# Sigmoid attention and a GELU feed-forward on one core: attention units two by two

## The chip, the core and the metric

The kernel runs on one core of one Trainium2 chip. The time is device microseconds of one execution; the kernel before has a median of 1010.88 us in three runs (1010.87 to 1011.01). The profile is one further execution, recorded by the hardware profiler.

Engines are named as the profile names them: PE (TensorE matmul), PEld (its weight loads), DVE (VectorE), ACT (ScalarE), POOL (GpSimd), SP (the queue that issues most loads).

## What is computed

```python
# q, k, v: (8 batches, 12 heads, 448, 64) fp32; w_in 768x2048, w_out 2048x768
scores = scale * np.matmul(q, k.transpose(0, 1, 3, 2)) - np.log(S)
attn = 1.0 / (1.0 + np.exp(-scores))
out = np.matmul(attn, v).astype(np.float32)
x = np.ascontiguousarray(out.transpose(0, 2, 1, 3)).reshape(B * S, H * D)   # 3584 x 768
h = x @ w_in
g = 0.5 * h * (1.0 + erf(h * inv_sqrt2))
return (g @ w_out).astype(np.float32)
```

## The kernel before

The program has two phases on the one core. The attention takes about the first 245 us, the feed-forward the rest. The change is in the attention alone; the feed-forward splits each product into seven smaller ones and stays as it is.

**Units.** Four heads of one batch make a unit; there are 24, three to a batch, and unit u belongs to batch u // 3. For each unit `scores` (L447) makes six score tiles of 128 keys x 2 x 448 queries, two head pairs by three key blocks. Each tile is three steps of two matmuls: q and k are split into a high part `hi` (a cast, L408) and a low part `lo` (raw minus `hi`, L417), and the steps are hi x lo, lo x hi and hi x hi. ACT turns each tile into probabilities with a sigmoid (L425), from PSUM into one of eight SBUF buffers `a`. The last 64 keys of all heads form one more tile, `sc_t` (`scores_tail`, L464), made from unsplit operands.

**Values.** `values(u)` (L480) multiplies probabilities and v into the PSUM tile `pav`, in two halves: first the tail and the three blocks with one wiring of the array's quarters, then the three blocks with the other. Between the halves DVE copies one column of `pav` into `ones`, the program's tile `mark` (L507); the second half waits for that copy. There too stands the score tail of the next unit.

**Parking.** After `values(u)` DVE copies the two halves of `pav` out (`park`, L531). From unit 6 on, each half goes into a buffer of `piece` (names `x6_0`, `x6_1` for unit 6), of which there are three in rotation, and from there by a DMA that POOL issues (L532) to the DRAM tile `scr_x`. Units 0 to 5 are copied mostly straight into SBUF tiles `x0_jk`, in halves (L525, L528).

**PSUM.** There are four tile places (`ps0` to `ps3`) of two banks each. Six score tiles go round over the four; `pav` and the next tail take two of them, and `place` exchanges third and fourth from unit to unit.

**Side work.** During the attention a `Decoder` rebuilds the weights from their raw bits in 20 chunks. A chunk has five steps: scale and place on ACT (L145, L156), a `post` step, then join (DVE, L175 and L183) and round (DVE, L190). Once two chunks are joined, `post` mixes their quarters with four DVE additions (`mix`, L107 to L110) and POOL issues seven DMAs of the results to DRAM (`scr_in`, L210). The table `STEPS` says how many steps come before `values` and how many inside, after the mark: (3, 2) for units 2 to 9 and 11 to 18, then (3, 1), (4, 1), (4, 1), (4, 0) for units 20 to 23. In unit 10 instead of it DVE combines quarters of the finished first rows of x (L564, L565: 128x1344 each), and in unit 19 it makes their low part (L568). `qk`, `v` and the raw weights are loaded by SP into three buffers each.

**Order.** Each engine runs its instructions in the order in which the Python code writes them. For a unit that is: six score tiles, splits of the next unit's q and k on DVE (the first pair's `hi` on ACT, in `idle`, for units up to 17), the decoder's steps, `values` with mark and tail, `park`, the next loads.

Of the kernel before, what the change touches and what calls it, by code (L numbers as in the profile page):

```python
# [17 lines left out]
P = 128  # L18
# [4 lines left out]
def tile_sigmoid_attention_gelu_ffn(  # L23
# [88 lines left out]

    def piece(name):
        return sb.tile([P, S], F32, tag="tmp", name=name, bufs=3)
# [7 lines left out]
    class Decoder:  # L122
        def __init__(self):
            self.raws, self.parts, self.rest, self.out = {}, {}, {}, None
            self.done = self.groups = self.closed = 0
            self.mixing, self.pending, self.open, self.second = [], [], [], None
            self.queue, self.next = nc.sync, None
            self.steps = self.work()
            self.taken = 0

# [69 lines left out]
        def post(self):  # L200
            some = bool(self.mixing or self.pending and self.second)
            while self.mixing:
                j, a = self.mixing.pop()
                s = sb.tile([P, 2, WU], F32R, tag="whl", name=f"sin{j}", bufs=WHL)
                s = s.bitcast(F32).rearrange("p a b -> p (a b)")
# [25 lines left out]
        def work(self):  # L231
# [3 lines left out]
            for i in range(len(CHUNKS)):  # L235
                self.scale(i)
                yield True
                self.place(i)
                yield True
# [8 lines left out]
            yield self.post()  # L248

# [20 lines left out]
    LATE = 17  # L270
    STEPS = {u: (3, 2) for u in (*range(2, 10), *range(11, 19))}
    STEPS |= {20: (3, 1), 21: (4, 1), 22: (4, 1), 23: (4, 0)}
    STEPS_IN_ALL = 5 * len(CHUNKS) + 2

    class Weights:
# [25 lines left out]
        def load_to(self, n, must=False):  # L301
            while self.loaded < min(n, len(self.units)):
# [4 lines left out]
                t = sb.tile([P, WU], F32, tag="wst", name=f"wst{i}", bufs=WST)  # L307
# [4 lines left out]
        def high_to(self, n):  # L312
            while self.ready < min(n, len(self.units)):
# [4 lines left out]
                hl = sb.tile([P, 2, WU], F32R, tag="whl", name=f"whl{i}", bufs=WHL)  # L318
# [55 lines left out]
    def attention(at, ps):  # L374
        raws, vals, parts, probs, pavs = {}, {}, {}, {}, {}
        total = B * NU

        def load(u):
            if u >= total:
                return  # L380
            b, n = divmod(u, NU)
# [36 lines left out]

        def sigmoid(u, p, c, sc, braided):
            a = at.tile([P, 2, S], F32, tag="a", name=f"a{u}_{p}_{c}", bufs=8)  # L420
            to = a
            if braided:
                to = a.rearrange("p j (a b) -> p j a b", a=2)
                sc = sc.rearrange("p j (b a) -> p j a b", a=2)
            nc.scalar.activation(to, sc, AF.Sigmoid, bias=NEG_LOG_S, scale=SCALE)  # L425
            probs[u, p, c] = a

        def place(u, n, name):
            third, fourth = (2, 3) if u % 2 == 0 else (3, 2)
            i = (0, 1, third, fourth, 0, 1, third, fourth)[n]  # L430
            return ps[max(i - 1, 0)].tile([P, 2, 512], F32, tag=f"ps{i}", name=name)[:, :, :S]

        def scores(u, p, c):
            if u >= total:
                return
            sc = place(u, FULL * p + c, f"sc{u}_{p}_{c}")
# [17 lines left out]
            sigmoid(u, p, c, sc, braided)  # L454
# [3 lines left out]
        def scores_tail(u):  # L458
# [3 lines left out]
            sc = place(max(u - 1, 0), 2 * FULL + 1, f"sc{u}_t")  # L462
# [10 lines left out]
        def values(u, meanwhile, idle):  # L473
            pav = pavs[u] = place(u, 2 * FULL, f"pav{u}")

            def chunk(c, swap):
                a = [probs[u, 0 if c == FULL else p, c] for p in range(2)]
# [11 lines left out]
            order = [0, 1, 2, FULL] if u == 0 else [FULL, 0, 1, 2]  # L489
            if u == total - 1:  # L490
                chunk(FULL, 0)
                for p in range(2):
                    for c in range(FULL):
                        for j in range(2):
# [3 lines left out]
                                probs[u, p, c][:, j],  # L498
# [6 lines left out]
            for c in order:  # L505
                chunk(c, 0)
            nc.vector.tensor_copy(mark, pav[:, :, 0])  # L507
            meanwhile()
            scores_tail(u + 1)
            idle()  # L510
            for c in range(FULL):
                chunk(c, 1)

# [29 lines left out]
        warm = place(0, FULL, "warm")  # L543
# [7 lines left out]
        for u in range(total):  # L551
            for p in range(2):
                for c in range(FULL):
                    scores(u, p, c)
            if u == 0:
                scores_tail(u)
# [5 lines left out]
            if u == 10:  # L562
# [3 lines left out]
            if u == 19:  # L566
# [3 lines left out]
            def meanwhile():  # L570
                if u == 0:
                    split_qk(1, 0)
                    split_qk(1, 1)
                decode(u, 1)
# [3 lines left out]
            def idle():  # L578
                if 2 < u + 2 <= LATE:
                    high_qk(u + 2, 0, nc.scalar.copy)  # L580
                if u == 10:
# [4 lines left out]
            values(u, meanwhile, idle)  # L586
# [7 lines left out]
            if u in (total - 6, total - 5):  # L594
                W.load_to(2 * (u - total + 7))

# [343 lines left out]
```

## Time and profile before

| what | us or share |
|---|---|
| median of three runs | 1010.88 |
| span of the profiled execution | 1009.3 |
| PE busy | 1004.9 (100%) |
| PEld busy | 909.3 (90%) |
| DVE busy | 705.4 (70%) |
| ACT busy | 678.8 (67%) |
| POOL busy | 105.0 (10%) |
| chain that ended last: PE | 95% |
| of it the scores (L447), the values (L480) and the tails (L464) | 9%, 13%, 2% |

The span runs from the first to the last instruction in the record; the run's time is 1.6 us above it. A timeline row gives a start, the time from there to the end of its last instruction, and how many instructions stand in it (xN); a bracket behind it says how long the engine had been idle and what released it. Matmuls overlap, so the difference of two starts says what a stretch costs PE, not the time of one row. One matmul of the order lists below is two records in the trace.

### The profile page before, as it was taken

How to read it: one execution, taken by the hardware profiler on the slowest of the kernel's cores; microseconds unless marked ns; L12 is line 12 of the kernel's file. 1: busy time of each engine (PE TensorE's matmuls, PEld its weight loads, DVE VectorE, ACT ScalarE, POOL GpSimd, SP SyncE). 2: the span in 40 equal slices, each digit the busy share in tenths (PEclk: the TensorE clock that was granted, in tenths of full speed). 3: DMA queues.
4: the chain of work that ended last, by engine and by line, in shares of the span. 5: the costliest groups of instructions: out<-in, count | busy, mean ns of one | idle time of the engine just before them, and what ended most of it. 6: DMA issues, size and time to landing. Idle time of an engine off the chain costs nothing.

```text
span 1009.3 us, 16521 instructions
## 1 busy us (share of the span) xinstructions
PE 1004.9 (100%) x6406; PEld 909.3 (90%) x6406; DVE 705.4 (70%) x834; ACT 678.8 (67%) x935; POOL 105.0 (10%) x168
## 2 busy tenths in 40 slices
PE   9999999999999999999999999999999999999998
PEld 5656666667999999999999999999999999999998
DVE  3677777777988987773378867534887774368873
ACT  5888887788886756567665655766656467666652
POOL 0122222233323210010000000100000000000000
PEclk9999999999999999999999999999999999999999
DMA  9899999998996765564344455634435543334441
GB/s 275 246 333 331 313 323 330 340 346 286 331 332 218 201 236 149 169 198 146 127 120 126 142 148 172 195 115 130 132 112 151 162 145 120 110 110 125 141 140 64
DMA packets 83214, 199.16 MB, mean 197 GB/s; under 512 B 9408, under 2 KB 33984, under 8 KB 83136
## 3 DMA queue, kind: packets, MB, share of 16 engines
q1 hardware_dynamic: 69360, 152.24, 49.3%
q0 software_dynamic: 11840, 39.23, 11.1%
q10 hardware_dynamic: 1936, 6.63, 1.9%
q8 instruction: 50, 0.82, 0.3%
q14 instruction: 28, 0.23, 0.1%
HBM read 156.10 MB, written 41.29 MB: 196 GB/s over the span
## 4 chain that ended last, share of the span: by engine, by line
PE 95%; DVE 2%; issue 2%; DMA 0%; ACT 0%; POOL 0%; DVEq 0%; POOLq 0%
PE pf L602 71%; PE pav L480 13%; PE sc L447 9%; PE sc_t L464 2%; DVE tmp L639 1%; DVE whl L326 0%; PE pav L495 0%; DMA scr_out<-wd 0%; PE warm L545 0%; POOL scr_out L219 0%; DVE wd L175 0%; DVE wd L190 0%; DVE xl_p L639 0%; DVE g L639 0%; ACT me L145 0%
## 5 line engine op out<-in xcount | busy, mean ns | idle before, releaser
L602 PE MATMUL pf<-op,whl 128*128 128x448 f32 x2016 | 382.1, 352 | 0.0
L602 PEld LDWEIGHTS pf<-op,whl 128*128 128x128 f32 x2016 | 380.9, 189 | 0.5 <-DVE op L639 0.2
L602 PE MATMUL pf<-xh_p,whl 128*128 128x448 f32 x1296 | 353.0, 353 | 0.1
L326 DVE TENSOR_TENSOR whl<-wst,whl 128x768 fp32r<-128x768 f32 x224 | 213.5, 954 | 153.6 <-ACT whl L319 153.2
L319 ACT CAST whl<-wst 128x768 fp32r<-128x768 f32 x224 | 186.0, 830 | 142.3 <-PE pf L602 124.5
L602 PEld LDWEIGHTS pf<-xh_p,whl 128*128 128x128 f32 x1296 | 244.9, 189 | 1.4 <-issue 0.7
L602 PE MATMUL pf<-xl_p,whl 128*128 128x448 f32 x624 | 219.9, 352 | 0.0
L425 ACT ACTIVATE a<-sc 128x896 f32<-128x896 f32 x144 | 119.2, 933 | 34.3 <-PE sc L447 34.2
L480 PE MATMUL pav<-a,v 64*64 64x448 f32 x1296 | 133.1, 541 | 0.0
L639 DVE TENSOR_TENSOR op<-g,op 128x896 fp32r<-128x896 f32 x112 | 121.3, 1084 | 0.9 <-ACT op L649 0.9
L602 PEld LDWEIGHTS pf<-xl_p,whl 128*128 128x128 f32 x624 | 117.9, 189 | 0.1
L480 PEld LDWEIGHTS pav<-a,v 64*64 64x64 f32 x1296 | 55.5, 132 | 61.0 <-issue 33.4
L649 ACT CAST op<-g 128x896 fp32r<-128x896 f32 x112 | 104.8, 936 | 1.7 <-PE pf L602 1.7
L639 DVE TENSOR_TENSOR g<-g,g 128x896 f32<-128x896 f32 x64 | 69.3, 1083 | 0.0
L636 ACT ACTIVATE g<-tmp 128x448 f32<-128x448 f32 x64 | 40.3, 631 | 38.2 <-DVE tmp L639 38.1
L636 ACT ACTIVATE g<-pf 128x448 f32<-128x448 f32 x64 | 34.8, 543 | 39.9 <-PE pf L602 39.7
L639 DVE TENSOR_TENSOR tmp<-pf,g 128x448 f32<-128x448 f32 x64 | 39.8, 623 | 26.3 <-PE pf L602 17.8
L351 POOL DMA_DIRECT2D x<-scr_x x24 | 18.0, 807 | 324.8 <-ACT g L746 204.2
L447 PE MATMUL sc<-lo,hi 64*128 64x448 f32 x276 | 51.2, 367 | 0.0
L417 DVE TENSOR_TENSOR lo<-qk,hi 128x896 fp32r<-128x896 f32 x46 | 50.1, 1088 | 1.1
L447 PE MATMUL sc<-hi 64*128 64x448 f32 x276 | 48.7, 349 | 0.0
L447 PE MATMUL sc<-hi,lo 64*128 64x448 f32 x276 | 48.7, 349 | 0.0
(75 smaller groups left out, 746.1 us busy)
## 6 DMA issues: line engine op xcount, KB each, us to landing
wst<-scr_in SPq DMA_DIRECT2D x112, 384.0 KB, 3.1
wst<-scr_out SPq DMA_DIRECT2D x112, 384.0 KB, 3.1
v<-v_dram SPq DMA_DIRECT2D x48, 256.0 KB, 7.9
raw<-w_in_dram SPq DMA_DIRECT2D x16, 767.8 KB, 6.0
out_dram<-tmp SPq DMA_DIRECT2D x47, 224.0 KB, 2.1
qk<-q_dram SPq DMA_DIRECT2D x23, 448.0 KB, 9.7
qk<-k_dram SPq DMA_DIRECT2D x46, 224.0 KB, 10.4
scr_out<-wd POOLq DMA_DIRECT2D x36, 256.0 KB, 5.2
```

What stands on the lines that cost most here:

```text
L319: nc.scalar.copy(hl[:, 0], t)
L326: nc.vector.tensor_tensor(hl[:, 1], t, hl[:, 0], op=ALU.subtract)
L351: queue.dma_start(dst[:, :, a], src[:, :, a])
L417: nc.vector.tensor_tensor(lo, raw, hi, op=ALU.subtract)
L425: nc.scalar.activation(to, sc, AF.Sigmoid, bias=NEG_LOG_S, scale=SCALE)
L447: nc.tensor.matmul(sc[:, j], ks[rows(j), 1, keys], braid(qs[rows(j), 0]) if braided else qs[rows(j), 0], start=n == 0, stop=n == last,)
L464: nc.tensor.matmul(sc[rows(p), j], raw[rows(j), p, 1, FULL * P :], raw[rows(j), p, 0], start=True, stop=True,)
L480: nc.tensor.matmul(pav[rows(j), p], vals[u][half, p, j, c], a[p][half, j], start=not swap and c == order[0], stop=c == (order[-1], FULL - ...
L602: nc.tensor.matmul(bank, a, braid(m), **flags)
L636: nc.scalar.activation(straight(dst), unbraid(src), AF.Gelu)
L639: nc.vector.tensor_tensor(out, a, b, op=op)
L649: nc.scalar.copy(op[:, 0], src)
```

## The change

The units 2 to 17 are now done two by two (`paired`), the others as before (`single`). For a pair u, u+1:

- twelve score tiles in one stretch, going round over the four PSUM places; then `values(u)` with its tail and parks, then `values(u + 1)` with its own;
- tiles 3 and 7 of the twelve are copied raw from PSUM to SBUF by DVE (`evict`), and ACT applies the sigmoid later in place (`late_sigmoid`, after tiles 8 and 11 are written in the code);
- of the four `hi` casts for the next pair, POOL does three and DVE one; ACT none;
- the decoder does ten steps per pair: three before each mark of `values` (join, round and what stands ahead), the scale and place of the next chunk ahead of time (`begin_next`), and the `post` in the middle of the first values;
- probabilities have 13 buffers: eight of their own, three in the weights' staging buffer `wst_all` and two in `whl1`, both idle at that time;
- both units park after their values, so four pieces per pair, in the same three `piece` buffers;
- the work on x of unit 10 moves to unit 19, that of unit 19 to unit 20; `STEPS` gives unit 18 (3, 0) and unit 19 none.

```diff
+        def weight_pair(n, name):
+            return sb.tile([P, 2, WU], F32R, tag=f"whl{n % 2}", name=name, bufs=WHL // 2)
 ...
-    STEPS = {u: (3, 2) for u in (*range(2, 10), *range(11, 19))}
-    STEPS |= {20: (3, 1), 21: (4, 1), 22: (4, 1), 23: (4, 0)}
+    PAIRED = range(2, 18, 2)
+    STEPS = {18: (3, 0), 20: (3, 1), 21: (4, 1), 22: (4, 1), 23: (4, 0)}
 ...
+        def begin_next(self):
+            i = self.next_chunk
+            self.scale(i)
+            self.place(i)
+            self.ahead.add(i)
+            self.taken += 2
 ...
+        def evict(u, p, c, sc):
+            a = occupy(u, p, c)
+            nc.vector.tensor_copy(ordered(a), sc.rearrange("p j (b a) -> p j a b", a=2))
+
+        def late_sigmoid(u, p, c):
+            a = probs[u, p, c][1]
+            nc.scalar.activation(a, a, AF.Sigmoid, bias=NEG_LOG_S, scale=SCALE)
 ...
-            if u == 10:
+            if u == SINGLE + 1:
                 x01, x11, x00 = (x0[jk].bitcast(F32) for jk in ((0, 1), (1, 1), (0, 0)))
                 nc.vector.tensor_tensor(x01, x11, x01, op=ALU.subtract)
                 nc.vector.tensor_tensor(x6, x01, x00, op=ALU.add)
-            if u == 19:
+            if u == SINGLE + 2:
                 lo = x0[0, 0]
                 nc.vector.tensor_tensor(lo, lo.bitcast(F32), h0, op=ALU.subtract)
 ...
-                if 2 < u + 2 <= LATE:
-                    high_qk(u + 2, 0, nc.scalar.copy)
 ...
+        def paired(u):
+            a, b, c, d = perm
+            begun = u > PAIRED[0]
+            after = [(u + 2, 0), (u + 2, 1)]
+            if u + 2 < SINGLE:
+                after.append((u + 3, 0))
+            load(u + 3)
+            load_v(u + 2)
+            tiles = [(w, p, c) for w in (u, u + 1) for p in range(2) for c in range(FULL)]
+            for n, at_tile in enumerate(tiles):
+                if n == FULL:
+                    high_qk(u + 1, 1, nc.vector.tensor_copy)
+                scores(*at_tile, perm[n % 4], evict if n in (3, 7) else sigmoid)
+                if n == 3:
+                    split_qk(u + 1, 1)
+                if n in (8, 11):
+                    late_sigmoid(*tiles[{8: 3, 11: 7}[n]])
+            for w, p in after:
+                high_qk(w, p, nc.gpsimd.tensor_copy)
+            split_qk(*after[0])
+            if begun:
+                dec.go(3)
+
+            def idle1():
+                load(u + 4)
+                dec.post()
+                if len(after) > 2:
+                    split_qk(*after[2])
+                dec.begin_next()
+
+            values(u, a, b, [FULL, 1, 2, 0], lambda: None, idle1)
+            for p in range(2):
+                park(u, p)
+            load_v(u + 3)
+            split_qk(*after[1])
+
+            def idle2():
+                load(u + 5)
+                dec.go(3)
+                dec.begin_next()
+
+            values(u + 1, c, d, [0, 1, 2, FULL], lambda: None, idle2)
+            for p in range(2):
+                park(u + 1, p)
 ...
+            if u in PAIRED:
+                paired(u)
+                a, b, c, d = perm
+                perm = (b, a, d, c)
+                u += 2
```

The order lists show the instructions of an engine as they stand in the program, with buffer numbers in the names; line numbers are those of the kernel before or of the changed one.

On PE, before, around the end of unit 6's score tiles: `sc6_1_2` is the last of its six tiles, `a6_...` are probabilities, `v6` the values.

```order
L447 MATMUL sc6_1_2_916<-lo6_1_813,hi6_1_812 128x448 x2
L447 MATMUL sc6_1_2_916<-hi6_1_812,lo6_1_813 128x448 x2
L447 MATMUL sc6_1_2_916<-hi6_1_812 128x448 x2
L480 MATMUL pav6_949<-a6_0_3_847,v6_750 64x448 x4
L480 MATMUL pav6_949<-a6_0_0_878,v6_750 64x448
L480 MATMUL pav6_949<-a6_1_0_905,v6_750 64x448
L480 MATMUL pav6_949<-a6_0_0_878,v6_750 64x448
L480 MATMUL pav6_949<-a6_1_0_905,v6_750 64x448
```

On PE, after, at the end of the stretch of units 6 and 7 (`a_all`, `wst_all` and `a_lent` are the probabilities' buffers):

```order
L482 MATMUL sc7_1_2_932<-lo7_1_864,hi7_1_863 128x448 x2
L482 MATMUL sc7_1_2_932<-hi7_1_863,lo7_1_864 128x448 x2
L482 MATMUL sc7_1_2_932<-hi7_1_863 128x448 x2
L518 MATMUL pav6_956<-a_all_128,v6_597 64x448 x16
L502 MATMUL sc7_t_974<-qk7_564 64x448 x4
L518 MATMUL pav6_956<-a_all_128,v6_597 64x448 x12
L518 MATMUL pav7_1022<-wst_all_109,v7_779 64x448
L518 MATMUL pav7_1022<-a_lent0_129,v7_779 64x448
```

Before, unit 6's six tiles are followed by its values; now twelve tiles of units 6 and 7 stand in a row, and the values of 7 follow those of 6 with nothing between.

On DVE, before, from the parks of unit 6 to those of unit 7 (`x6_0` is a `piece`, `pav6` the values, `ones` the mark, `wd` and `raw` the decoder's):

```order
L531 COPY x6_0_995<-pav6_949 128x448
L531 COPY x6_1_998<-pav6_949 128x448
L417 TENSOR_TENSOR lo8_0_981<-qk8_807,hi8_0_980 128x896
L408 CAST hi8_1_1063<-qk8_807 128x896
L417 TENSOR_TENSOR lo8_1_1064<-qk8_807,hi8_1_1063 128x896
L507 COPY ones_63<-pav7_1070 128x2
L175 SCALAR_TENSOR_TENSOR wd4_967<-raw5_720,me5_1067 128x768
L183 TENSOR_SCALAR raw5_720<-raw5_720 128x768
L190 ISA wd4_967<-raw5_720,wd4_967 128x1536
L531 COPY x7_0_1115<-pav7_1070 128x448
L531 COPY x7_1_1118<-pav7_1070 128x448
```

On DVE, after, from the parks of unit 6 on; `a_all<-sc8_1_0` is the raw copy of tile 3 of the next stretch:

```order
L572 COPY x6_0_1012<-pav6_956 128x448
L572 COPY x6_1_1015<-pav6_956 128x448
L448 TENSOR_TENSOR lo8_1_945<-qk8_741,hi8_1_944 128x896
L545 COPY ones_63<-pav7_1022 128x2
L179 SCALAR_TENSOR_TENSOR wd4_1050<-raw4_715,me4_997 128x768
L187 TENSOR_SCALAR raw4_715<-raw4_715 128x768
L194 ISA wd4_1050<-raw4_715,wd4_1050 128x1536
L572 COPY x7_0_1071<-pav7_1022 128x448
L572 COPY x7_1_1074<-pav7_1022 128x448
L439 CAST hi9_1_1104<-qk9_807 128x896
L461 COPY a_all_128<-sc8_1_0_1107 128x896
L448 TENSOR_TENSOR lo9_1_1105<-qk9_807,hi9_1_1104 128x896
```

The parks of unit 6 and of unit 7 are now one `lo`, one mark and one decoder step apart, and the parks of unit 7 stand ahead of the last `hi` cast and of the raw copies of the next stretch.

On DVE, before, ahead of the mark of unit 20 (`sin7` is the result of a mix):

```order
L417 TENSOR_TENSOR lo21_1_2685<-qk21_2435,hi21_1_2684 128x896
L107 TENSOR_TENSOR sin7_2691<-wd14_2347 128x384
L108 TENSOR_TENSOR sin7_2691<-sin7_2691,wd14_2347 128x384
L109 TENSOR_TENSOR sin7_2691<-wd14_2347 128x384
L110 TENSOR_TENSOR sin7_2691<-wd14_2347,sin7_2691 128x384
L507 COPY ones_63<-pav20_2703 128x2
```

On DVE, after, at the same place (`x0_00` is the quarter of x whose low part is made):

```order
L448 TENSOR_TENSOR lo21_1_2553<-qk21_2247,hi21_1_2552 128x896
L107 TENSOR_TENSOR sin7_2559<-wd14_2251 128x384
L108 TENSOR_TENSOR sin7_2559<-sin7_2559,wd14_2251 128x384
L109 TENSOR_TENSOR sin7_2559<-wd14_2251 128x384
L110 TENSOR_TENSOR sin7_2559<-wd14_2251,sin7_2559 128x384
L611 TENSOR_TENSOR x0_00_111<-x0_00_111,xh0_p1_114 128x1344
L545 COPY ones_63<-pav20_2572 128x2
```

The subtraction on x (128x1344) now stands between the mix and the mark.

## Rows read from the trace of the kernel before

**Rows 1.** page, section 1 and section 4 (the chain that ended last):

```profile
PE 1004.9 (100%) x6406; PEld 909.3 (90%) x6406; DVE 705.4 (70%) x834; ACT 678.8 (67%) x935; POOL 105.0 (10%) x168
PE 95%; DVE 2%; issue 2%; DMA 0%; ACT 0%; POOL 0%; DVEq 0%; POOLq 0%
```

**Rows 2.** windows view: stretch, PE, PEld, DVE, ACT, POOL busy, PEclk, DMA share:

```profile
80.00:100.00 20.00, 20.00 (x208) 12.28 (x201) 14.79 (x23) 17.10 (x22) 6.40 (x11) 1.00 0.95 326
```

**Rows 3.** timeline of PE, units 7 and 8: start us, us, line, operation:

```profile
79.46 0.35 PE L447 MATMUL sc<-hi 64*128 64x448 f32 x2
79.75 3.27 PE L480 MATMUL pav<-a,v 64*64 64x448 f32 x32
82.80 0.96 PE L464 MATMUL sc_t<-qk 64*64 64x448 f32 x8
83.55 2.46 PE L480 MATMUL pav<-a,v 64*64 64x448 f32 x24
85.95 0.46 PE L447 MATMUL sc<-lo,hi 64*128 64x448 f32 x2
86.24 0.35 PE L447 MATMUL sc<-hi,lo 64*128 64x448 f32 x2
89.27 0.35 PE L447 MATMUL sc<-hi 64*128 64x448 f32 x2
89.55 3.27 PE L480 MATMUL pav<-a,v 64*64 64x448 f32 x32
```

**Rows 4.** groups by line and shape, 0 to 245 us: busy, mean ns:

```profile
L531 DVE COPY x<-pav 128x448 f32<-128x448 f32 x36 | 20.7, 616 | 9.5 <-PE pav L480 5.7 <-PE pav L495 3.8
L408 DVE CAST hi<-qk 128x896 fp32r<-128x896 f32 x31 | 19.2, 619 | 0.1
L408 ACT CAST hi<-qk 128x896 fp32r<-128x896 f32 x15 | 14.0, 931 | 1.0 <-DMA qk<-k_dram 1.0
L425 ACT ACTIVATE a<-sc 128x896 f32<-128x896 f32 x144 | 119.2, 933 | 34.3 <-PE sc L447 34.2
```

**Rows 5.** timeline of ACT, unit 8 (columns as in rows 3):

```profile
86.83 4.96 ACT L425 ACTIVATE a<-sc 128x896 f32<-128x896 f32 x6 [1.26 <-PE sc L447]
```

**Rows 6.** timeline of DVE, unit 8:

```profile
89.88 0.55 DVE L107 TENSOR_TENSOR sin<-wd 128x384 f32<-128x384 f32 x1
91.41 0.55 DVE L110 TENSOR_TENSOR sin<-wd,sin 128x384 f32<-128x384 f32 x1
92.88 0.16 DVE L507 COPY ones<-pav 128x2 f32<-128x2 f32 x1 [0.91 <-PE pav L480]
93.50 0.96 DVE L175 SCALAR_TENSOR_TENSOR wd<-raw,me 128x768 uint32<-128x768 uint32 x1 [0.46 <-DMA scr_x<-x]
95.97 1.15 DVE L531 COPY x<-pav 128x448 f32<-128x448 f32 x2
97.03 1.08 DVE L417 TENSOR_TENSOR lo<-qk,hi 128x896 fp32r<-128x896 f32 x1
```

**Rows 7.** timeline of POOL (DMA issue), unit 8:

```profile
96.88 1.07 POOL L532 DMA_DIRECT2D scr_x<-x  x2 [1.71 <-DVE x L531]
```

**Rows 8.** the tile scr_x, 60 to 240 us: issue to landing:

```profile
DMA to landing us min/median/max: 2.3/7.2/8.5
```

**Rows 9.** DMA issues, 60 to 180 us: count, KB each, median us to landing:

```profile
scr_x<-x POOLq DMA_DIRECT2D x22, 224.0 KB, 7.0
```

**Rows 10.** timeline of DVE, unit 10:

```profile
109.49 1.55 DVE L564 TENSOR_TENSOR x<-x,x 128x1344 f32<-128x1344 f32 x1
111.08 1.56 DVE L565 TENSOR_TENSOR x_p<-x,x 128x1344 f32<-128x1344 f32 x1
112.55 0.15 DVE L507 COPY ones<-pav 128x2 f32<-128x2 f32 x1
```

**Rows 11.** timeline of PE, unit 10:

```profile
112.97 2.46 PE L480 MATMUL pav<-a,v 64*64 64x448 f32 x24
```

**Rows 12.** timeline of DVE, unit 20:

```profile
210.68 0.16 DVE L507 COPY ones<-pav 128x2 f32<-128x2 f32 x1 [0.35 <-PE pav L480]
```

More of the change, by code (lines that the diff above doesn't have):

```diff
@@ L235, in work @@
             for i in range(len(CHUNKS)):
[L236 to L239, printed above, removed]
+                if i not in self.ahead:
+                    self.scale(i)
+                    yield True
+                    self.place(i)
+                    yield True
+                self.next_chunk = i + 1
                 yield self.post()
@@ L376, in attention, with occupy, vacate @@
         total = B * NU
+        SINGLE = PAIRED[-1] + 2
+        loaded = set()
+        own = at.tile([P, 8, 2, S], F32, name="a_all", bufs=1)
+        lent = [wst_all[:, n * 2 * S : (n + 1) * 2 * S] for n in range(3)]
+        for n in range(2):
+            m = weight_pair(1, f"a_lent{n}").bitcast(F32)
+            lent.append(m.rearrange("p a b -> p (a b)")[:, : 2 * S])
+        lent = [m.rearrange("p (j s) -> p j s", j=2) for m in lent]
+        vacant = [(True, own[:, n]) for n in range(8)] + [(False, m) for m in lent]
+        def occupy(u, p, c):
+            slot = next(s for s in vacant if s[0] or u < SINGLE)
+            vacant[:] = [s for s in vacant if s is not slot]
+            probs[u, p, c] = slot
+            return slot[1]
+        def vacate(u, p, c):
+            vacant.append(probs.pop((u, p, c)))
         def load(u):
-            if u >= total:
+            if u >= total or u in loaded:
                 return
+            loaded.add(u)
             b, n = divmod(u, NU)
@@ L471, in scores_tail, with values @@
             sigmoid(u, 0, FULL, sc, False)
-        def values(u, meanwhile, idle):
-            pav = pavs[u] = place(u, 2 * FULL, f"pav{u}")
+        def values(u, i, tail, order, meanwhile, idle):
+            pav = pavs[u] = place(i, f"pav{u}")
             def chunk(c, swap):
-                a = [probs[u, 0 if c == FULL else p, c] for p in range(2)]
+                a = [probs[u, 0 if c == FULL else p, c][1] for p in range(2)]
                 for p, j in QUARTERS:
@@ L584, in idle @@
                     W.high_to(W.ready + 1)
-            values(u, meanwhile, idle)
+            order = [0, 1, 2, FULL] if u == 0 else [FULL, 0, 1, 2]
+            values(u, perm[2], perm[3], order, meanwhile, idle)
             for p in range(2):
```

69 lines of the change are left out of this document (41 added, 28 removed).

## The prediction

> **What bounds the kernel now.** I read the page first: PE is busy in the whole span and 95% of the chain that ended last is PE [rows 1]. Between 80 and 100 us PE is busy 20.00 of 20 us at a granted clock of 1.00, DVE 14.79, ACT 17.10, and the DMA engines 0.95 [rows 2]. So a change in the attention gains only what PE itself loses, and it costs whatever makes PE wait. The DMA engines have no room to catch up.
>
> The timeline of PE shows what a unit costs. I write S for the start of its first score tile and V for that of its first values. From V to V it is 89.55 - 79.75 = 9.80 us [rows 3]. A score step costs (89.27 - 86.24)/16 = 0.189; a values record costs (83.55 - 82.80)/8 = 0.094. Eighteen steps and 64 records make 3.40 + 6.01 = 9.41. The missing 0.39 sits at the changes between scores and values: the last score step lasts 79.75 - 79.46 = 0.29 (0.10 too long) and the 32 records behind it 3.05 (0.05 too long); the 24 records ahead of the next scores 85.95 - 83.55 = 2.40 (0.15 too long) and the first score step 0.29 (0.10 too long) [rows 3].
>
> **The sum is made against the profiled execution.** Its span is 1009.3 and the median 1010.88, 1.6 above it; what the change adds to or takes from the span I add to the median.
>
> **1. Shape changes removed: -3.1 us.** A pair has one stretch of scores and one of values where it had two of each: 8 x 0.39 = 3.1. This is all that there is to gain.
>
> **2. Score places in a stretch of twelve: 0.3 per stretch.** ACT takes six tiles in 4.96, one in 0.93 [rows 4, 5], a pace of 0.81; PE makes one in 3 x 0.189 = 0.57. Tile n needs the place of tile n - 4. The first sigmoid starts at 86.83 = S + 0.88 [rows 3, 5], so tile 2 is out at S + 0.88 + 2 x 0.81 + 0.93 = S + 3.43. Tile 6 begins at S + 0.10 + 18 x 0.189 = S + 3.50, and its weights are loaded a step earlier, S + 3.31: 0.1 to 0.15 late. Tile 10 waits for tile 6 and loses as much again. DVE takes tiles 3 and 7; a copy of 128x448 out of PSUM costs 0.616 [rows 4], so 128x896 at most 1.23. Tile 3 is written by about S + 2.6, out by S + 3.8, and tile 7's weights are due at S + 3.88, just in time. I take 0.3 for a stretch in which nothing else holds PE up, and between 0 and 0.5.
>
> **3. The park buffers: 1.4 us at six boundaries, the largest term.** There are three `piece` buffers, and a pair now parks four pieces. The fourth, x7_1 for units 6 and 7, takes the buffer of x6_0, so its copy waits until the DMA of x6_0 has landed. Before, two pairs of pieces were a unit apart as well, but nothing on PE's path stood right behind the copy. Now tile 3 of the next stretch goes into the place of `pav7`, which is free only when x7_1 is out.
>
> When does x6_0 leave? On DVE the mark is at V + 92.88 - 89.55 = V + 3.33; behind it now stand the mix (89.88 to 91.41 + 0.55, so 2.08) and one `lo` (1.08) [rows 6]. The copy of x6_0 therefore starts near V + 6.5; POOL issues its DMA 96.88 - 95.97 = 0.91 later [rows 6, 7], at V + 7.4. The values of two units take (85.95 - 79.75 - 0.25) + 6.20 = 12.1 [rows 3], so this is S - 4.7, S being the next stretch's start. The landing takes 7.0 at the median between 60 and 180 us [rows 9], 2.3 to 8.5 with a median of 7.2 to 240 us [rows 8]. The copy of x7_1 adds 0.62 [rows 4] and some 0.05 of signalling. Tile 3's weights are due at S + 0.10 + 9 x 0.189 - 0.19 = S + 1.61. PE so waits by landing - 5.6: nothing at 5.6, 1.4 at 7.0, 2.9 at 8.5. I take 7.0: the DMA engines stay as full as they are, and the pieces leave shortly after a mix's seven DMAs.
>
> Behind the waiting copy on DVE stand the `hi` cast of (u + 1, 1), the raw copies of tiles 3 and 7 and two `lo`; all of them serve tiles that PE reaches only after tile 3, so they move with it. A wait of 1.4 also lets ACT catch up, which takes away term 2 in that stretch.
>
> Pieces go to `scr_x` from unit 6 on; of pair 4 and 5 only one half needs a piece. The boundaries ahead of units 8, 10, 12, 14, 16 and 18 remain: 6 x 1.4 = 8.4, and between 0 and 17. The stretches of units 2, 4 and 6 pay term 2: 3 x 0.3 = 0.9.
>
> **4. Work moved to units 18 to 20: 1.9 us.** A mark is late when DVE's list ahead of it is too long. In unit 10 the two additions on x (109.49 to 112.55, 3.06) end just in time: the mark has no idle time ahead of it, yet the second half starts at 112.97, three units of 9.81 after 83.55 [rows 3, 10, 11]. Unit 19 gets the same two with one more cast on DVE (0.62 and a gap) ahead of them: 0.6 late. In unit 20 the mark stands behind two splits and a mix and idles 0.35 [rows 12]; now a subtraction of 1.59 (111.08 - 109.49) [rows 10] comes between: 1.2 late. Unit 18 has join and round in place of the mix, 95.97 - 93.50 = 2.47 for 2.08 [rows 6]: 0.1. Together 1.9, between 1.5 and 2.3. The mark of unit 10 is relieved, but it cost nothing.
>
> **5. Casts on GpSimd: nothing, with a wide bound.** The trace shows no tensor work on POOL. The nearest rows are the same cast on DVE, 0.62, and on ACT, 0.93 [rows 4]. In a stretch the third cast can start when tile 11 is out, about V; the first `lo` is wanted by DVE about S + 6, the third at V + 5.4. The casts become late at some 3 us each; POOL's own queue behind them (the DMAs of `scr_in` and the parks) is not wanted before V + 4. I take 0.93, hidden. Rival B below is the case in which they cost DVE something.
>
> **6. At nothing.** ACT loses its casts and keeps 14 sigmoids a pair. The decoder's scale and place stand behind the stretch's sigmoids, join wants them only at the next mark. DVE gets two raw copies for one cast less, 1.6 to 1.9 per pair of 19.6, with 14.79 of 20 busy now [rows 2]. The loads of q and k have three buffers still; those of unit u + 3 may land in the stretch of u, and are wanted at V + 5.4, over 12 us after S, where the longest landing of a piece is 8.5 [rows 8].
>
> **Sum.** -3.1 + 0.9 + 8.4 + 1.9 = +8.1, so 1010.9 + 8.1 = **1019.0 us**.
>
> **The rivals.**
>
> B, DVE and GpSimd hinder each other. DVE's list from S to the mark: parks 0.7, cast 0.65, then raw copy of tile 3 to about S + 3.7, `lo` 1.0, raw copy 1.1, `lo` 1.0, join and round 2.47, so S + 9.4 [rows 4, 6]; the mark may be as late as V + 3.4 = S + 10.4. The slack is 1.0. If two of the three casts, 0.93 each, hold DVE up in full, a mark is 0.9 late, in eight pairs 6.9 in all: 1019.0 + 6.9 = 1026. Against it: nothing in the trace of before shows two engines in each other's way here, since POOL moves no data there; for it: three casts fall into the fullest part of DVE's list. The Trainium skill speaks for B (page "SBUF — State Buffer", section "Who interferes with whom"): GpSimd's one read and one write port are VectorE's second pair, shared under an exclusive lock. No run here shows it yet; by it the time would be nearer 1026, without it 1019.
>
> C, the parks land in time, no more than slightly slower. If x6_0 lands within 5.6, term 3 is nothing and term 2 is paid in all eight stretches: -3.1 + 2.4 + 1.9 = +1.2, 1012.1. For it: landings go down to 2.3 [rows 8]. Against it: the median is 7.0 with the DMA engines full, and nothing in the change lightens them. It decides at a landing of 5.6.
>
> D, the clean gain: ACT's tiles come in time, since the 0.15 of term 2 is of the size of the signalling I put in, the parks land early, and unit 19 and 20's lists run shorter: 1010.9 - 3.1 = 1007.8. It needs three terms at their lower ends.
>
> E, a cast on GpSimd costs more than 3 us. Then `lo` comes late and the mark with it: two casts a pair stand ahead of a `lo` that is wanted, so each us above 3 moves DVE's list by some 2 us per pair, 16 in all at 4 us: 1035.
>
> That the change does not do what it says is no rival: the order list has the twelve tiles in a row and one change of shape per pair.
>
> **How the numbers follow.** The forecast has 0.47 (landings of 6 to 8, 1013 to 1025), B 0.21, C 0.17, D 0.10, E 0.05. The predicted time is the forecast's, 1019.0. For 8 in 10 the range must take in C and most of B, and leave out D and E: 1010 to 1029. Within 0.2% is within 2.0 us, about what a measurement of this kernel can tell from no change. D is faster; C at 1012.1 is the same; the rest is slower: 0.10, 0.17, 0.73.
>
> **What would show it.** In the profile after: between values of a pair 12.1 from V to the next S, and one long last score step per pair (term 1). On PE a gap ahead of tile 3 in the stretches from unit 8 on, on DVE idle time ahead of the second L572 copy released by a DMA of `scr_x` (term 3); none ahead of units 4 and 6. Gaps of 0.1 to 0.2 ahead of tiles 6 and 10 in the stretches of 2, 4 and 6 (term 2). Late marks in 19 and 20 (term 4). The row of L439 on POOL gives the cast's price, and DVE rows L439, L448 and L461 longer than 0.62, 1.08 and 1.2 would show B. I am wrong if the DVE copies of the parks run without waiting, or if marks in the pairs come late.

## The result and the profile after

The changed kernel takes 1024.63 us, the median of four runs (1022.18 to 1025.64), the kernel before 1010.92 in the same comparison. The ratio is 1.0134, 95% interval 1.0119 to 1.0148: 13.7 us slower, where +8.1 was forecast and 1010 to 1029 given as the range. The profiled execution has a span of 1022.6, 13.3 above that of before, and its own time is 1024.35.

The page of the changed kernel, its sections 1 and 4, against [rows 1]:

```profile
PE 1007.7 (99%) x6406; PEld 903.8 (88%) x6406; DVE 724.9 (71%) x842; ACT 667.5 (65%) x920; POOL 128.8 (13%) x191
PE 85%; DMA 8%; DVE 2%; POOL 2%; issue 2%; SPq 0%; POOLq 0%; ACT 0%; DVEq 0%
```

PE's share of the chain falls from 95% to 85%; 8% of it is now DMA, which had none (the pieces 4%, the loads of q and k 3%, raw weights 1%, by the same section). The view of waits for 60 to 200 us (who waits for whom: us in all, times, longest) says which. The row of PE:

```profile
PE sc L482 <- DVE x L572: 9.8, 6, 2.3
```
And the row of DVE:

```profile
DVE x L572 <- DMA scr_x<-x: 12.3, 6, 2.7
```

Six times a score tile waits for a park copy, and six times a park copy waits for the DMA of an earlier piece. The chain of 84 to 92 us shows one of the six from end to end (start us, us, what):

```profile
80.44 8.21 DMA scr_x<-x
88.65 0.02 issue
88.67 0.64 DVE x L572
89.31 0.14 issue
89.44 2.60 PE sc L482 x17
```

The DMA of `x6_0` is issued at 80.44 and lands 8.21 us later; only then does DVE copy `x7_1` into the same buffer (0.64), and only then may PE begin tile 3 of the next stretch. The timeline of PE there, to be read against [rows 3]:

```profile
86.91 0.35 PE L482 MATMUL sc<-hi 64*128 64x448 f32 x2
89.44 0.46 PE L482 MATMUL sc<-lo,hi 64*128 64x448 f32 x2 [2.18 <-DVE x L572]
89.71 0.38 PE L482 MATMUL sc<-hi,lo 64*128 64x448 f32 x2
...
91.09 0.64 PE L482 MATMUL sc<-hi,lo 64*128 64x448 f32 x2
91.47 0.64 PE L482 MATMUL sc<-hi 64*128 64x448 f32 x2
...
94.04 0.38 PE L482 MATMUL sc<-lo,hi 64*128 64x448 f32 x2
94.23 0.38 PE L482 MATMUL sc<-hi,lo 64*128 64x448 f32 x2
...
96.43 2.10 PE L518 MATMUL pav<-a_all,v 64*64 64x448 f32 x19
```

The row of 86.91 is the last step of tile 2; the next step starts 2.53 later instead of 0.19. A second thing is in these rows: from 91.09 to 91.47 a step costs 0.38, and by 94.04 it costs 0.19 again. The windows (columns as in [rows 2]) tell why:

```profile
88.00:90.00 2.00, 0.56 (x6) 0.59 (x8) 1.16 (x2) 0.70 (x1) 0.41 (x1) 1.00 1.06 387
90.00:92.00 2.00, 2.00 (x18) 2.00 (x16) 1.69 (x2) 0.92 (x1) 0.13 (x1) 0.64 1.04 295
92.00:94.00 2.00, 2.00 (x14) 2.00 (x12) 0.40 (x1) 1.65 (x2) 0.96 (x1) 0.50 1.09 267
94.00:96.00 2.00, 2.00 (x24) 2.00 (x24) 1.73 (x2) 1.35 (x3) 0.94 (x1) 1.00 0.96 375
```

The granted clock is 0.50 between 92 and 94, that is 1.2 instead of 2.4 GHz. It was 1.00 in [rows 2].

Where the 13.3 us went, by the starts of the matmuls in the trace:

| part | us |
|---|---|
| changes between scores and values, eight of each fewer | -3.1 |
| waits ahead of tile 3 at the six boundaries (start to start, less one step of 0.19): 2.35, 1.91, 1.03, 0.95, 2.43, 2.06 | +10.7 |
| low clock behind two of them: from tile 3 to the first values 6.99 instead of 5.36, twice | +3.3 |
| late score places, and restarts behind the waits, all stretches | +1.5 |
| late marks in units 18, 19, 20: 0.05, 0.39, 0.70 | +1.1 |
| a late second mark in the pair of 2 and 3 (behind unit 4's score tail) | +0.3 |
| unit 1 starts earlier, 16.62 instead of 16.98 (16.50 to 17.68 in the experiments, so scatter) | -0.4 |
| sum | +13.4 |

### The profile page after: what moved, and what is told of

It is laid out like the page before. It is cut to its first block, busy times and chain, and to the rows that moved or that the text cites. A ratio compares the mean times of both kernels' runs of the same rounds, so it can differ in the third digit from the quotient of the medians.

```text
span 1022.6 us, 16579 instructions
## 1 busy us (share of the span) xinstructions
PE 1007.7 (99%) x6406; PEld 903.8 (88%) x6406; DVE 724.9 (71%) x842; ACT 667.5 (65%) x920; POOL 128.8 (13%) x191
## 4 chain that ended last, share of the span: by engine, by line
PE 85%; DMA 8%; DVE 2%; POOL 2%; issue 2%; SPq 0%; POOLq 0%; ACT 0%; DVEq 0%
PE pf L704 75%; PE sc L482 5%; PE pav L518 5%; DMA scr_x<-x 4%; DMA qk<-k_dram 3%; POOL scr_in L213 2%; DMA raw<-w_in_dram 1%; DVE lo L448 1%; PE sc_t L502 1%; PE pav L532 0%; DMA qk<-q_dram 0%; DVE x L572 0%; POOL hi L439 0%; SPq L422 0%; DVE hi L439 0%
## 5 line engine op out<-in xcount | busy, mean ns | idle before, releaser
L338 DVE TENSOR_TENSOR whl<-wst_all,whl 128x768 fp32r<-128x768 f32 x224 | 213.7, 955 | 153.7 <-ACT whl L331 153.3
L331 ACT CAST whl<-wst_all 128x768 fp32r<-128x768 f32 x224 | 186.0, 830 | 142.4 <-PE pf L704 124.5
L518 PE MATMUL pav<-a_all,v 64*64 64x448 f32 x936 | 104.4, 541 | 0.7 <-DVE ones L545 0.7
L457 ACT ACTIVATE a_all<-sc 128x896 f32<-128x896 f32 x91 | 77.6, 930 | 26.3 <-PE sc L482 26.3
L518 PEld LDWEIGHTS pav<-a_all,v 64*64 64x64 f32 x936 | 37.5, 132 | 50.0 <-issue 38.5
L482 PE MATMUL sc<-lo,hi 64*128 64x448 f32 x276 | 54.6, 380 | 9.8 <-DVE x L572 9.8
L448 DVE TENSOR_TENSOR lo<-qk,hi 128x896 fp32r<-128x896 f32 x46 | 53.8, 1170 | 5.9 <-POOL hi L439 5.4
L482 PE MATMUL sc<-hi 64*128 64x448 f32 x276 | 51.8, 359 | 0.0
L482 PE MATMUL sc<-hi,lo 64*128 64x448 f32 x276 | 51.7, 359 | 0.0
```

What stands on the lines that cost most here:

```text
L331: nc.scalar.copy(hl[:, 0], t)
L338: nc.vector.tensor_tensor(hl[:, 1], t, hl[:, 0], op=ALU.subtract)
L448: nc.vector.tensor_tensor(lo, raw, hi, op=ALU.subtract)
L482: nc.tensor.matmul(sc[:, j], ks[rows(j), 1, keys], braid(qs[rows(j), 0]) if braided else qs[rows(j), 0], start=n == 0, stop=n == last,)
L518: nc.tensor.matmul(pav[rows(j), p], vals[u][half, p, j, c], a[p][half, j], start=not swap and c == order[0], stop=c == (order[-1], FULL - ...
```

## The experiments

Each time is the device time of the slowest core. The kernel before was run beside each; its medians lay between 1010.65 and 1011.39, so each experiment is set against the one run beside it. The indented text is what was expected before the run. Two buffers (e3), casts twice (e4) and one buffer (e10) were executed once, the others ten to twelve times.

### A fourth buffer for the pieces (e1)

```diff
-            x = piece(f"x{u}_{p}")
+            x = x6[:, u % 3] if p and u - 1 in PAIRED else piece(f"x{u}_{p}")
```

The tile `x6` lies idle until unit 19.

> The changed kernel, but the second half of a pair's second unit (x7_1 for units 6 and 7) parks in a free third of the tile x6 and no longer in the buffer of x6_0, so its copy waits for no landing. Theory (park buffers): the six gaps on PE ahead of tile 3, 10.7 us in the profile of the changed kernel, go, and with them the two falls of the granted clock behind the longest of them (3.4); each of the eight stretches then pays about 0.2 for late score places: 1024.6 - 10.7 - 3.4 - 0.4 + 1.2 = about 1011.3. Rival (GpSimd's casts hold DVE up): the copy's wait only hid the late marks; with it gone the marks of the pairs come 0.3 to 0.9 late and the time stays at 1014 to 1018.

Measured: 1011.53, ratio to before 1.0008 (0.9998 to 1.0017). DVE's timeline at the boundary of units 7 and 8, and the first mark of the next pair; below it, on PE, the first score steps of the pairs from 8 and from 10 on:

```profile
86.16 0.62 DVE L572 COPY x<-pav 128x448 f32<-128x448 f32 x1 [0.26 <-PE pav L518]
86.70 0.61 DVE L572 COPY x_p<-pav 128x448 f32<-128x448 f32 x1
...
96.53 0.16 DVE L545 COPY ones<-pav 128x2 f32<-128x2 f32 x1 [0.53 <-PE pav L518]
```

```profile
86.00 0.46 PE L482 MATMUL sc<-lo,hi 64*128 64x448 f32 x2
105.42 0.46 PE L482 MATMUL sc<-lo,hi 64*128 64x448 f32 x2
```

The two park copies (the second into `x_p`, the room of `x6`) follow each other without a wait, and the mark still finds DVE idle for 0.53. The clock is 1.0 throughout. About 13 of the 13.7 us were this one buffer, the low clock behind it included. All pairs follow each other at 19.42 us, where two units took 19.61 (85.95 [rows 3] to 105.56): the 0.39 of the shape changes less 0.20 for the score places. The rival (late marks behind the casts) finds nothing here: no mark of a pair is late.

### Two buffers instead of three (e3)

The changed kernel, with

```diff
-        return sb.tile([P, S], F32, tag="tmp", name=name, bufs=3)
+        return sb.tile([P, S], F32, tag="tmp", name=name, bufs=2)
```

> The changed kernel with two piece buffers for three. Theory (park buffers): x7_1 now waits for the landing of x6_1, which comes 0.6 to 1.0 us after that of x6_0, so each of the six gaps grows by about 0.85, 5 us in all; gaps above some 2.2 us are followed by the low clock, four instead of two, another 3.4: about 1033. Rival (the gaps come from something else, GpSimd's casts or late q and k): nothing changes, 1024 to 1026.

Measured: 1033.25. The tile `scr_x`, 60 to 240 us, in the list of who waited for it (us, times), and a row of the view of waits of the whole execution:

```profile
  DVE x L572: 17.8, 10
```

```profile
DVE tmp L741 <- DMA out_dram<-tmp: 11.1, 8, 2.5
```

The six waits on PE are 2.60, 2.59, 1.72, 1.69, 2.75 and 2.73, 14.1 in all, 3.4 more than in the changed kernel; 5 was expected. The time was met for two further reasons. Here 1.7 and 1.3 us went lost at the first marks of units 2 and 3, where GpSimd's casts waited for q and k. And the edit does more than it was meant to: `piece` also makes the feed-forward's tiles `tmp`, and DVE now waits there for the store of an earlier one (the second row; the changed kernel has no such wait), and from the last values on the execution takes 2.7 us more, 770.05 instead of 767.38. So the sign and the place are shown by the six waits in the trace, and the close agreement of the total is chance. The clock fell behind two of the six waits, not four.

### The work on x0, first attempt (e2)

```diff
-            if u == SINGLE + 1:
-                x01, x11, x00 = (x0[jk].bitcast(F32) for jk in ((0, 1), (1, 1), (0, 0)))
-                nc.vector.tensor_tensor(x01, x11, x01, op=ALU.subtract)
-                nc.vector.tensor_tensor(x6, x01, x00, op=ALU.add)
-            if u == SINGLE + 2:
+            if u == SINGLE + 1:
                 lo = x0[0, 0]
 ...
                 decode(u, 1)
+                if u == SINGLE:
+                    x01, x11, x00 = (x0[jk].bitcast(F32) for jk in ((0, 1), (1, 1), (0, 0)))
+                    nc.vector.tensor_tensor(x01, x11, x01, op=ALU.subtract)
+                    nc.vector.tensor_tensor(x6, x01, x00, op=ALU.add)
```

The part behind `decode(u, 1)` stands behind the mark.

> As e1, and the work on x0 put elsewhere: the two additions (3.1 us) behind the mark of unit 18, the low part (1.6 us) ahead of the mark of unit 19, so that unit 20 is as it was before the change. Theory: the three late marks (0.05, 0.39 and 0.70 in the changed kernel) go, 1.1 us less than e1, about 1010.2. Rival: DVE's list behind the mark of 18 is then too long, the parks of unit 18 leave late and tile 3 of unit 19 waits instead; the time stays that of e1.

Measured: 1011.57, as without it. The timeline of DVE from the mark of 18 on, in an execution of 1014.15, the longest of the ten:

```profile
192.24 1.55 DVE L618 TENSOR_TENSOR x<-x,x 128x1344 f32<-128x1344 f32 x1
195.84 1.56 DVE L619 TENSOR_TENSOR x_p<-x,x 128x1344 f32<-128x1344 f32 x1 [2.05 <-DMA scr_x<-x_p]
197.31 1.15 DVE L572 COPY x<-pav 128x448 f32<-128x448 f32 x2
```
And PE at tile 3 of unit 19:

```profile
198.61 0.46 PE L482 MATMUL sc<-lo,hi 64*128 64x448 f32 x2 [1.67 <-DVE x L572]
```

The late marks are gone, but the second addition writes `x6`, in which the fourth piece still lies: it waits 2.05 for that piece's landing, the parks behind it leave late, and tile 3 of unit 19 waits 1.84. The rival's end came true by a wait that my own buffer had put there. This execution also lost 1.5 and 1.2 us at the first two marks of the pairs, which e1's had not.

### The work on x0, one piece to a slot (e5)

One addition behind the mark of 18, one ahead of the mark of 19, the low part behind that mark.

```diff
+            if u == SINGLE + 1:
+                nc.vector.tensor_tensor(x6, x01, x00, op=ALU.add)
 ...
                 decode(u, 1)
+                if u == SINGLE:
+                    nc.vector.tensor_tensor(x01, x11, x01, op=ALU.subtract)
+                if u == SINGLE + 1:
+                    lo = x0[0, 0]
+                    nc.vector.tensor_tensor(lo, lo.bitcast(F32), h0, op=ALU.subtract)
```

> As e2, where the two additions behind the mark of unit 18 made tile 3 of the next unit wait 1.84 us for the parks, with the work spread: one addition behind the mark of 18, one ahead of the mark of 19, the low part behind that mark, so that no slot of some 3 us takes more than 1.6. Theory (each mark and each park has its own due time, and 1.6 fits into either slot): no late mark in 18 to 20 and no gap ahead of tile 3, 1.1 us less than e1: 1010.4. Rival (the moved work was not what cost): 1011.5 as e1 and e2.

Measured: 1010.12, ratio 0.9995 (0.9986 to 1.0004). No late mark in 18 to 20 and no gap ahead of tile 3; 1.4 less than e1, though each has an interval of some 0.9 us to either side and they ran beside different executions of the kernel before. The trace shows the term gone; the time agrees with the 1.1 that stood there.

### Casts twice (e4)

```diff
                 high_qk(w, p, nc.gpsimd.tensor_copy)
+                nc.gpsimd.tensor_copy(parts[w, p][0], raws[w][:, p])
```

> As e1, with each of the three casts on GpSimd done twice in a row (same source, same target). In e1 a cast on GpSimd lasts 0.94 alone and 1.66 beside a subtraction of DVE, one `lo` per pair lasts 1.53 instead of 1.08, and DVE still waits 0.53 ahead of the first mark. Theory (the engines get in each other's way, and the slack hides it): with twice the casts the `lo` that wait for them come 0.9 later and one more is lengthened by 0.45; less the slack of 0.5 a mark is 0.4 to 0.9 late in eight pairs: 1015 to 1019. Rival (casts are hidden whatever they cost): 1011.5, as e1.

Measured: 1020.75, 9.2 above e1, more than I expected. DVE's timeline ahead of the first mark of units 6 and 7:

```profile
74.76 1.78 DVE L448 TENSOR_TENSOR lo<-qk,hi 128x896 fp32r<-128x896 f32 x1 [0.40 <-POOL hi L660]
76.47 1.68 DVE L179 SCALAR_TENSOR_TENSOR wd<-raw,me 128x768 uint32<-128x768 uint32 x1
78.18 1.17 DVE L187 TENSOR_SCALAR raw<-raw 128x768 uint32<-128x768 uint32 x1
79.39 1.56 DVE L194 CUSTOM_DVE_ANT_0 wd<-raw,wd 128x1536 uint16<-128x1536 uint16 x1
```
POOL beside it, where L660 is the second cast:

```profile
73.79 0.94 POOL L660 CAST hi<-qk 128x896 fp32r<-128x896 f32 x1
75.67 1.67 POOL L660 CAST hi<-qk 128x896 fp32r<-128x896 f32 x1
```
And PE at the second half of the values, which that mark holds up:

```profile
81.08 2.49 PE L518 MATMUL pav<-a_all,v 64*64 64x448 f32 x24 [1.59 <-DVE ones L545]
```

The four operations of DVE last 1.78, 1.68, 1.17 and 1.56, against 1.08 and 0.96 for the first two in [rows 6] and 0.57 and 0.96 for the others in e1's profile, 2.6 more in all; POOL's cast grows from 0.94 to 1.67 in the same stretch. PE's row idles 1.59, its start 1.77 late; nine marks are late by 0.35 to 1.81, 9.9 together. So the casts are near free only while they fit: DVE's slack ahead of a pair's first mark is the 0.53 that it idles there in e1. In the changed kernel, where the parks come late, it idles there in three pairs of eight only.

### The start: raw loads later (e6, e11), then spread (e8)

The expectations of e2 and e3 did not foresee the first pair's waits. In e2's profile POOL's timeline reads:

```profile
36.74 1.80 POOL L439 CAST hi<-qk 128x896 fp32r<-128x896 f32 x2 [8.31 <-DMA qk<-k_dram]
42.45 0.93 POOL L439 CAST hi<-qk 128x896 fp32r<-128x896 f32 x1 [3.91 <-DMA qk<-k_dram]
```

Casts for units 4 and 5, made during the pair of 2 and 3, wait for k until 36.7 and 42.4; the subtractions and that pair's marks come late behind them. Ahead of these loads stand three raw loads of 768 KB on SP. The first attempt issues all three a unit later (`dec.go(1)` after unit 1):

> As e5, with the first three loads of raw weights (768 KB each) issued after unit 1 instead of after unit 0, so that q and k of unit 4 are not queued behind them. In the profiles of e2 and e3 GpSimd's casts for units 4 and 5 waited for q and k, and the first two marks came 1.2 to 1.7 us late each; in e1 they did not. Theory: these waits differ from run to run and go here: median 0 to 1 us below e5, 1009.6 to 1010.4, and no run above 1011.5. Rival: the weights then come late and the first join waits: 1011 or more.

Measured: 1010.59, ratio 1.0004 (0.9993 to 1.0016), runs from 1009.37 to 1015.27. Missed on both counts: unit 4's cast was in time in the profiled execution, but now unit 5's q and k stood behind the raw loads, and the second mark came 0.51 late. The three longest runs, 1013.96 and up, had a mean clock of 0.998 and the others 0.999 to 1.000, which points to a stretch at half the clock in each; no trace of one was kept. The second attempt issues one after unit 1, one behind the loads of unit 5, one behind those of unit 6:

```diff
-            for i in range(3):
-                self.load(i)
+            self.load(0)
 ...
+            if not begun:
+                dec.load(1)
 ...
                 load(u + 4)
+                if not begun:
+                    dec.load(2)
```

> As e6, with the three first loads of raw weights spread: one after unit 1, one behind the loads of unit 5, one behind those of unit 6. In e6 the cast for unit 5 waited for q and k behind three raw loads and the second mark came 0.5 late; runs lay between 1009.4 and 1015.3. Theory (late q and k at the start): no late mark in the first pair, median 1009.2 to 1009.8 and the upper runs gone. Rival (the spread has another cause): median and spread as e6.

Measured: 1009.47, runs from 1009.19 to 1010.90, ratio 0.9983 (0.9974 to 0.9992): faster than the kernel before, and without the long runs of e6. Whether the loads alone would have brought that:

> The kernel before with the first three loads of raw weights issued after unit 1 instead of after unit 0, and nothing else. Asked: whether the gain of e8 over the kernel before comes from the pairs or from the loads alone. In the profile of the kernel before the units from 2 on follow each other at 9.81 to 9.87, so the start holds nothing up there. Theory (the gain is that of the pairs, 8 x 0.2 = 1.6): no difference, within 0.5 us of the kernel before. Rival (the loads alone bring it): 1 to 1.5 us less than the kernel before.

Measured: 1010.81 beside 1010.75, ratio 1.0001 (0.9992 to 1.0010). The kernel before gains nothing from e6's form of the loads; e8's form was not tried on it. The gain of e8, 1.9, fits that of the pairs once their waits are gone, 8 x 0.2 = 1.6 us.

### Tiles 2 and 5 evicted (e7, e9)

```diff
-                scores(*at_tile, perm[n % 4], evict if n in (3, 7) else sigmoid)
+                scores(*at_tile, perm[n % 4], evict if n in (2, 5) else sigmoid)
```

It builds on e6. The fourth `hi` goes into the idle tile `h0`, cast on GpSimd; both late sigmoids come after tile 8, and the first values take their blocks in another order.

> As e6, with tiles 2 and 5 copied out raw by DVE instead of 3 and 7, both late sigmoids after tile 8, and the fourth `hi` cast also on GpSimd (into a free tile), so that DVE is free for tile 2 at once. By the pace of 0.81 a tile on ACT all places are then free in time but one (0.1 late), where e1's stretches lose 0.22 each. Theory (score places): 8 x 0.12 to 0.22 less than e6, 1008.5 to 1009.4, faster than the kernel before by 0.1 to 0.2%. Rival (more casts on GpSimd lengthen DVE's list): marks late by up to 0.4, 8 x 0.4 more, 1012.

Measured: 1011.29, ratio 1.0005 (0.9996 to 1.0014), not the 1008.5 to 1009.4 expected. The pairs do follow each other faster, at 19.34 instead of 19.42 (0.08, not 0.12 to 0.22), but the first pair lost 1.46 ahead of tile 9 (start to start, less one step; the next expectation has 1.28) and 0.81 at a mark. With the loads of e8 and the first pair's cast a unit earlier:

> As e7, with the raw loads of e8 and the first pair's cast of (3, 1) made a unit earlier. In e7 the pairs follow each other at 19.34 instead of 19.42, but the first pair lost 1.28 ahead of tile 9 (its cast and `lo` came late) and 0.81 at a mark. Theory: both go, 1011.3 - 2.1 = 1009.2, with 8 x 0.08 = 0.6 below e8. Rival (the fourth cast on GpSimd costs elsewhere what the places give): no better than e8.

Measured: 1009.84, ratio 0.9982 (0.9974 to 0.9991), beside e8's 0.9983. It beats the kernel before, but the 0.6 over e8 can't be seen: inconclusive. The tile 9 of the first pair still lost 0.56.

### One buffer (e10)

The changed kernel with `bufs=1` in the line of the second experiment.

> The changed kernel with a single piece buffer: each parked piece waits for the landing of the one before, so the copies of a pair leave some 8.5 us apart and PE waits 10 to 20 us at each of the six boundaries: 1090 to 1150. Asked here is the granted clock: behind waits of 2.35 and 2.43 us (changed kernel) and 2.59 and 2.73 (e3) it fell to half for about 3 us, behind 2.60 and 2.75 (e3) and all waits up to 2.06 it did not. Theory (a wait of PE brings it, the length alone does not settle it near 2.5 us): behind each of the long waits the clock is at half. Rival (the falls came from something else in those stretches): after long waits the clock stays at 1.0 in most.

Measured: 1193.93, above the range. Of the 169.6 us by which the profiled span exceeds that of the changed kernel, 124.0 lie in the attention (its last values record starts at 379.24 instead of 255.21), where not only the boundaries but marks too waited, 4.3 to 7.5 us at a time. The other 45.6 lie in the feed-forward, whose `tmp` tiles have one buffer too; DVE's wait of e3's second row is 32.7 us there, in 14 times. Without the 45.6 the time would be some 1148 (an estimate from these spans), inside the range. A window of the attention (columns as in [rows 2]):

```profile
100.00:115.00 15.00, 7.32 (x50) 2.91 (x42) 4.70 (x7) 4.22 (x6) 1.08 (x2) 0.77 0.83 288
```

The mean granted clock is 0.77 there, and below 1.00 in every stretch of the attention that holds such a wait.

## Why the prediction was right, and where it was off

The sign, the place and the mechanism were right: the time fell into the range, and the largest term was the one that was forecast to be. The 5.6 us by which it was too low are the landing (2.3) and the clock behind it (3.3); the smaller errors nearly cancel. Point by point.

**Shape changes, -3.1.** Right. e1 shows 19.42 per pair, 0.19 below two units, which is 0.39 less the 0.20 of the next term.

**Score places, 0.3 per stretch.** The mechanism is right, 0.20 to 0.22 measured in the stretches of units 2, 4 and 6. That a longer wait in a stretch makes up for it was not right: behind the waits some 0.16 per stretch remain, 0.08 of it the restart.

**The park buffers, 8.4.** The step is right, its size was a fifth too small: 10.7. The formula, landing less 5.6, holds within 0.35, always on the high side. What was off is the landing. I took 7.0, a median of first and second pieces; the six first pieces took 8.21, 7.56, 6.80, 6.65, 8.20 and 8.01, a median of 7.8; none came under the 5.6 at which rival C would have won. Four of the six lie in the upper half of [rows 8], whose upper end is 8.5, so that row held the risk, but no row of before singles this piece out: it leaves 0.6 to 1.4 us behind the last DMA of a mix, and the pieces of before that come next behind one (1.1 to 4.4 us later, up to 190 us) landed in 5.75 to 7.42. Whether the mix is what makes it slower was not tested. "The boundaries of units 4 and 6 pay nothing" is right.

**The clock, missing from the sum.** I wrote that the work behind the waiting copy moves with it. It does, but two of the waits were followed by a stretch at half the clock, 1.6 us each and 3.3 in all. The rows of before could not price that: there PE never waited and the clock was 1.00 [rows 2]. The Trainium skill (page "TensorE: Matmul & The Clock Gate", section "Part 1: The HAM clock gate (the "warmup" mystery)") says that idling lets the array's clock fall to half. This case's trace agrees, with 0.50 between 92 and 94 us. I had not weighed it; yet behind the waits of 0.95 to 2.06 in the changed kernel the clock did not fall, so at the 1.4 that I forecast the term would have been nothing. It came with the longer landings.

**Units 18 to 20, 1.9.** Places right, size too large: 1.1 (0.05, 0.39, 0.70 for 0.1, 0.6, 1.2). DVE's timeline at the mark of unit 20:

```profile
222.79 1.55 DVE L611 TENSOR_TENSOR x<-x,xh_p 128x1344 fp32r<-128x1344 f32 x1
224.25 0.16 DVE L545 COPY ones<-pav 128x2 f32<-128x2 f32 x1
```
And PE behind that mark:

```profile
224.47 1.73 PE L518 MATMUL pav<-a_all,v 64*64 64x448 f32 x16 [0.53 <-DVE ones L545]
```

The mark starts 7.99 after the unit's first score tile (216.26). Before it was 6.99 (203.69 to the 210.68 of [rows 12]), so it is 1.00 later in its unit, where I had 1.24: the subtraction takes 1.46 to the start of the next operation, and the 1.59 that I used is its time to another of its kind [rows 10]. Of the 1.00, PE pays 0.70, since the second half can follow 0.22 after the mark's start, which left 0.2 of slack in the unit that I had called just in time (112.55 and 112.97 [rows 10, 11]). e5 takes the term away. No row shown gives the 0.1 for unit 18.

**Casts on GpSimd, nothing.** Right in the sum, and rival B's mechanism exists; but its price, 6.9, was not paid. The groups of the changed kernel up to 260 us (busy, mean ns):

```profile
L439 POOL CAST hi<-qk 128x896 fp32r<-128x896 f32 x23 | 26.4, 1149 | 40.7 <-PE sc L482 24.6 <-DMA qk<-k_dram 14.8 <-DVE lo L448 1.1
L448 DVE TENSOR_TENSOR lo<-qk,hi 128x896 fp32r<-128x896 f32 x46 | 53.8, 1170 | 5.9 <-POOL hi L439 5.4
L461 DVE COPY a_all<-sc 128x896 f32<-128x896 f32 x8 | 8.7, 1092 | 2.4 <-PE sc L482 2.4
```

A cast took 1.15 on the mean: 0.93 to 0.94 where it ran alone or had begun ahead of the `lo` beside it, 1.66 where the `lo` was already running. In the first case the `lo` was the one that took longer, 1.53 and once 1.78, which raises its mean from 1.08 in [rows 6] to 1.17. So the one that began second paid. The raw copies out of PSUM lasted 1.09 each, whatever ran beside them. That agrees with the rule of the page "SBUF — State Buffer" of the Trainium skill, section "Who interferes with whom": a VectorE instruction with two SBUF inputs contends with GpSimd's reads, one with at most one SBUF input, outside the two-port modes, does not. (L187, with one SBUF input, took 1.17 in e4's rows for 0.57; whether it ran in such a mode no run shows.) The extra 0.45 per pair stayed inside DVE's slack (e1), and twice the casts went beyond it (e4). My point of decision, a cast of 3 us, was too high: in e4 a cast done twice took 2.5 in all on the mean, and e4 paid 9.2.

**What I costed at nothing and should not have:** the loads of q and k at the start. The casts that the first pair makes for the next wait for loads queued behind 2.3 MB of raw weights. That cost 0.3 in this profile, the only late mark in a pair, 2.7 in e2's and 3.0 in e3's, and it is one reason why the runs of the paired kernels spread more than those before: with the loads spread (e8) the longest of eleven took 1010.90.

## What to carry to other kernels

When two stages are fused into one longer stretch, count the buffers that their side paths share: the same number in rotation holds half as long, and a copy that no one stood behind may now stand ahead of the engine that bounds the kernel. Price a wait on a DMA by the landing of just that transfer at just that place, not by the median of its kind, and add what the array's clock loses behind it. When an experiment takes a buffer away, look for every other user of it: here the feed-forward paid part of e3's and e10's time. Before moving small work off a busy slot, write down each slot's due time: here 3.1 us did not fit where twice 1.6 did.

## What the runs showed of the hardware that was not expected

PE's clock fell to half behind waits that were short: 2.35 and 2.43 us in the changed kernel, 2.59 and 2.73 with two buffers. Length alone did not settle it, as four windows with two buffers, each behind one wait, show (2.60, 2.59, 2.75 and 2.73 us):

```profile
92.00:96.00 4.00, 3.34 (x36) 3.37 (x38) 3.36 (x5) 1.90 (x3) 2.32 (x3) 1.00 1.09 278
114.00:118.00 4.00, 3.40 (x20) 3.43 (x22) 3.08 (x4) 0.92 (x1) 1.42 (x2) 0.61 1.08 305
180.00:184.00 4.00, 3.55 (x38) 3.58 (x40) 3.33 (x5) 2.11 (x3) 2.00 (x2) 1.00 1.08 227
202.00:206.00 4.00, 3.46 (x26) 2.45 (x30) 3.93 (x6) 2.48 (x3) 0.85 (x2) 0.71 1.10 244
```

The clock is 1.00, 0.61, 1.00 and 0.71. Three waits of e10 near this length, 2.36, 2.35 and 2.40 us, which end at 344.45, 358.37 and 370.65, say the same: the clock falls behind the first and the third. The last row shows a fall behind two short waits in its feed-forward (PE idle for 1.73 us up to 530.80 and for 0.70 up to 531.96):

```profile
344.00:352.00 8.00, 7.55 (x62) 4.85 (x66) 5.36 (x8) 4.85 (x5) 0.54 (x1) 0.79 0.31 86
358.00:364.00 6.00, 5.63 (x58) 3.23 (x62) 5.69 (x9) 4.66 (x5) 0.54 (x1) 1.00 0.60 194
370.00:376.00 6.00, 5.35 (x32) 2.92 (x34) 4.67 (x6) 4.37 (x5) 3.51 (x5) 0.72 0.64 197
532.00:534.00 2.00, 2.00 (x6) 1.85 (x7) 2.00 (x3) 1.90 (x3) 0.00 (x0) 0.56 0.73 238
```

Apart from those two it never fell behind waits up to 2.06; behind the 4.3 to 7.5 of e10 each stretch shows less than 1.00. A fall cost 1.6 us each time in the changed kernel. Nor does it come in every execution: the fastest of the four of the changed kernel, 1022.18, had a mean clock of 1.000, the profiled one 0.997. What decides between 2.3 and 2.8 us stays open.
